# A hand-written order of 946 operations replaced by another, from operation 87 on

## Chip, cores and metric

The kernel runs on one core of one Trainium2 chip. The metric is the device time of one execution in microseconds, as the median of several runs.

## The reference, cut to what matters

Attention with four sink positions and a window of 128, then an MLP whose activation is the square of a relu:

```python
# q, k, v: (4, 8, 768, 64) = batch, heads, sequence, head size; n_sink 4, window 128
scores = q @ k^T / sqrt(64)
keep = (pos_k < 4) | (0 <= pos_q - pos_k < 128)
a = softmax(where(keep, scores, -1e9))
x = (a @ v) as (4 * 768, 8 * 64) = 3072 tokens x 512
h = x @ w_in                # 512 -> 2048
out = (max(h, 0) ** 2) @ w_out    # 2048 -> 512, float32
```

## The kernel before, in words

The work is cut by batch b (0 to 3) and by slab s (0 to 2) of 256 query positions. The heads lie in four pairs m. For a slab, TensorE (PE) makes the scores of two head pairs at a time into two PSUM banks (L613); ScalarE (ACT) takes the exp of each bank (L634); a mask cuts the window's triangles, either on VectorE (DVE, L643 and L646) or on GpSimd (POOL, L218); PE multiplies with the values (L682); DVE normalises (L698 reciprocal, L699 product) into the tile xn_sb. The four sink positions have a small product (L572) and exp (L580) of their own, with "sink values" prepared ahead (L554: four small sums on POOL). The attention output has to be transposed for the MLP. For batches 0 and 1 PE does it (L731, copied out at L192 by ACT or L194 by DVE); for batches 2 and 3 the DMA does it, one tile of 128 positions per issue from SyncE's (SP's) queue (L713, xn_sb to xT). The inputs q and k are also transposed: by PE (L507) for batches 0 and 1, and by DMA from SP's queue (L461, qn to qkT) for batches 2 and 3. POOL's queue issues the loads (L308 w_in, L316 w_out, L372 and L403 q and k, L381 and L415 v). Each queue has eight semaphores for its transfers, so an issue waits until the one eight before it has landed.

The MLP's first layer is done partly in the classic form (L763 products, relu L775 on ACT or L777 on DVE, square L784 or L786) and partly by a scheme with seven instead of eight block products (a "quad", L894): sums of blocks of the input (L852; for some a copy "xd" on ACT, L192, comes first) and of the weights (L810, L818), seven products, and between them partial results t on DVE (L936; the first of them a copy on ACT or DVE), a relu for two of the four blocks (ACT L951 or DVE L953), a fused relu step for the others (L963), squares (ACT L917 or DVE L919). The second layer also goes by sums of squares (L1207), sums of weights (L1025), seven products of eight matmuls each (L1233; classic L984; the last slab has a form of its own, L1094), and its output quarters are copied out (L192, L194) or added (L1247), and stored by SP (L1276).

What sets the order is a table, `ORDER`, at the top of the file: 946 words, one for each operation. `Plan.run` issues the operations in the order of the table. The number of a word names the operation. A letter behind it (p, d, a, g) picks PE, DVE, ACT or POOL for an operation that can run on several, without one it takes the first of its list. `+0` and `+1` pick, for each PSUM slot that the operation takes, the pool "att" or "den"; each has two rooms of two banks. Since each engine works its queue in order, the table fixes the order of every queue, the engine of each movable operation, and which room is free when. A product that takes a room waits for the last reader of what was there.

```python
word, *chosen = word.split("+")
n = int(word.rstrip("pdag"))
o = self.ops[n]
o.engine = names[word[-1]] if word[-1] in names else next(iter(o.engines))
for s in o.takes:
    if len(s.pools) > 1:
        s.pool = s.pools[int(chosen.pop(0))]
    s.room = free[s.pool].pop(0)
o.run(o.engine)
```

The operations that the steps below name, by their number in the table:

| op | what it is |
|---|---|
| 35, 36; 127 | loads of the last two parts of w_out; the making of the masks (POOL) |
| 106, 118 | masks of batch 0, slab 1 |
| 208, 452 | sink values of batches 1 and 2 |
| 128, 166, 171, 282 | transpose of q and k, relu, product of layer 1, product of layer 2, all of batch 0 |
| 183, 184, 185 | last classic product of layer 1, its relu (ACT), its square (DVE) |
| 219, 230; 222, 233, 220, 231 | score products of batch 1; their exps |
| 301; 304, 305 | a sum of squares (DVE); first products of layer 2 of batch 0, slab 2 |
| 369, 383; 271, 273 | relus of two quads; copies of the transposed attention output |
| 389, 390, 408 | xd copy (ACT), sums of it (DVE), first product of a quad that uses them (batch 1, slab 2) |
| 397, 399; 400, 401 | t of a quad; products that need them |
| 454, 459 | sink product of batch 2, an exp |
| 468, 469 | product with the values and norm, batch 2, slab 0 |
| 406, 507 | a fused relu step L963 of a quad, a sum of squares |
| 472, 479 / 495, 488 | score products of batch 2, slab 1 / slab 2 |
| 486, 487, 502, 503; 594 | DMA transposes L713 of batch 2, slabs 1 and 2; sums of xT (L852) that need them |
| 680 to 683 | DMA transposes L461 of q and k of batch 3 |
| 648, 650; 704 | a relu and the product that needs it, batch 2; a score product of batch 3 |

Of the kernel before, what the change touches and what calls it, by code (L numbers as in the profile page):

```python
# [18 lines left out]


ORDER = """
944 0 1 2 7 8 9 10 11 12 13 14 15 16 17 18 945+0 3 5 19 20 21 6 79 22 23 24 25 55d 56d 57+0 58 59d 60a 83+0 85 103+1
105 26 27 28 62d 61d 63+1 64 67d 68d 65a 69+0 70 71d 72d 66a 84+1 73a 74a 75+1 76 78d 91+0 86 77a 93 80 113+1 87+0
92+1 89 94 95+0 97 115 88 90 96 98 114+1 99+0 101 117 100d 104+0 81+1 102d 107 82 4 29 106g 30 31 32 33 34 35 36 37 38
39 40 41 42 43 44 45 46 127 47 48 49 50 116d 118d 108d 156+0 109+1 119+1 121 111 162+0 110 120 122 112 123+1 125 124d
126d 157a 163a 158a 164a 168+1 165+0 51 52 53 54 177+0 169a 170d 208g 166a 167a 178d 171+1 179a 172a 128+1 131+0 174+0
173a 132a 129d 319 323 321 175d 324 176d 322 130a 320 159+1 133a 160a 161a 278+0 279 136+1 144+0 145+0 280 281 148 138
146 289+1 149d 139d 274 147d 275 282 290 283 291 292 284 276 277 134+1 137+0 135 286a 140 141d 285 287d 293 150+0 151
294 142+1 196+0 192+1 295 143 193 200+1 198a 202a 195d 197 199d 201 203d 297d 194d 296 298a 152+1 154 204+0 205
212+0+1 153a 155d 189+0 215 206a 213 190a 214 207d 186+0 216 191d 248+0 187d 249d 251+1 209 253a 188d 252a 180+1 181d  # L30
250d 182d 183+0 326 184a 185d 300 301 230+0+1 233 299 288 219+0+1 231 220 304+0 210+0 306a 211 222 305 237+0+0 240
232d 325 302 221 303 223 241d 238 239d 311 307 217+1 254+0 224+0 308a 255 309 218 242+0 225 243 452g 422 423 424 425
426 427 428 429 430 431 432 433 434 234g 235+1 226+0 228 310a 227a 229a 314 236 244+0 246 316a 247a 327 313 245d 329
256+0+1 257 315 328 332 317 330 347+1 333+1 348 334 259 335a 337 312 336 331 338 349a 263+1+1 266 264 339 351 340 341a
350 352 435 436 437 258g 438 439 267g 265g 361+0 353 362 354 363d 260g 364 343 365 366 445 440 453 444 441 355a 356a
342a 448 446 449 442 447 443 451 450 318 344 345 357 375+0 358 376 261+0 359 377a 346a 367 368 379 378 262 380 268+0
# [6 lines left out]
477+0 500+0 485 478 559 501 561 527+0 528 529d 563 562 493+0 565 558d 494 534 530 535 531d 566+0 567 532 533a 568d 569  # L43
564 570 572 571 536 683 682 677 678 486 502 680 711+0+0 487 503 573 574d 537 538 539d 540 681 541 560 714 712 704+0+0
580+0 581 576 577 582d 583 594 584 585 575a 705 707 688+0+0 713g 715g 706g 708g 689 691 578 586 587 626+1 627 588a
628a 612+0 686+0 613 687 630 596 692 690 595 629 631 716+0 717 589a 614a 632 633 579a 634a 635a 615 590 616 597 617
693+0 694 591 618 636 619 637 592 598+1 599 620a 600a 638 593a 601 622 640+0 641 602 623 642a 736 643 603 644 604 646
605 645 709+0 647 624 740+0 639a 621a 606a 648a 742a 649a 607a 608 609 738 737 650 651 743 739 710 610 611d 741
695+0+0 744a 625a 696 698 652 653d 755 697 699 756 757 745 747 746a 749 748 720+0+0 723 759+0 750 700+0 701 761a 762
751 721 752a 763a 760 722g 753 724g 727+0+1 774 775 758 728 730 725+0 766 764 778+1 779 765a 729d 767 776 726 777 768  # L50
731g 732+1 733 718 719 702 703 754 734 735 793 794 785 770 769 798+1 812+0 799 813 780a 771a 800a 814a 781 782a 797
796 786 772 795 815 801 802 816 817 818 803 783 819 784d 787 820a 804 805 789 822 823 829 826 827 828 791 806a 807a
821a 808 809 788 830+0 831 790a 832a 824 825d 810 858+1 811a 834 872+0 844+1 860a 846a 874a 833 835 836 837 873 845
859 876 838a 839a 886 887 888 875 877 861 840 841 848 862 864 792 773 842 863 847 889 849 878 879 890+0 865 843a 880a
850 882 883 851 892a 881a 866d 867d 884 893 894d 868 869 852a 853a 854 855 870 856 895 891 897 896a 885a 900 857d 871d
905 909+1 899 907 901 924 926 906 898 925 903 911a 912 913a 902a 928+1 904 914 910 929 931+1 915d 908 927 918 920 919
930a 933a 916 922 921d 934 917 923 932 935 936 939 937 938 943 940 942 941
"""
DUMMIES = {
    945: 29, 58: 8, 63: 10, 64: 4, 83: 3, 91: 3, 97: 3,  # L60
# [1340 lines left out]
```

## Time and profile before

| | us |
|---|---|
| runs shown | 210.41, 210.48, 211.18 |
| median | 210.48 |
| profiled execution, first to last instruction (span) | 208.3 |
| median less span | 2.2 |
| DVE busy | 173.1 |
| ACT busy | 135.9 |
| POOL busy | 96.4 |

The profile shows one execution. The span runs from its first to its last instruction. A line of a group names the source line, the engine, the operation, the tile written and the tiles read, the count, and then the busy time in all, the mean of one in ns, and the engine's idle time just before them with what ended it. A line of the windows gives, for a stretch of time, the busy time of each engine in the order PE, PEld (weight loads, beside PE), DVE, ACT, POOL, with the count of instructions, then the granted clock, the DMA share and the rate. A line of the waits gives who waited for whom, the time in all, how often, and the longest. In a timeline, the square bracket holds the idle time ahead of the row and what ended it.

### The profile page before, as it was taken

To read this page: it belongs to the slowest core of one execution; us is meant where nothing else is said; L and a number is where in the kernel's file an instruction comes from. 1 tells how busy PE (TensorE), PEld (TensorE's weight loads), DVE (VectorE), ACT (ScalarE), POOL (GpSimd) and SP (SyncE) were. 2 spreads that over 40 slices of the span, in tenths; PEclk is the share of its full clock that TensorE was granted. 3 is DMA by queue.
4 is the path that set the end of the run, shared out by engine and by line. 5 is a ranking of instruction groups with operands and counts; after the bars stand their busy time and mean duration, and the time that the engine had idled before them with its cause. 6 is when DMAs were issued, how large, how long until landed. Compare 5 with 4: busy or idle time off the path is not lost.

```text
span 208.3 us, 5924 instructions
## 1 busy us (share of the span) xinstructions
PE 200.5 (96%) x2476; PEld 174.3 (84%) x2476; DVE 173.1 (83%) x318; ACT 135.9 (65%) x189; POOL 96.4 (46%) x138
## 2 busy tenths in 40 slices
PE   7989999999998999999999998999999999999993
PEld 7658997457986889989878987999888999998893
DVE  6759268867599998999999987999989598999933
ACT  2695888433749589999987047988856248693110
POOL 7999274599599976689356209000043000000000
PEclk9999999999999999999999999999999999999999
DMA  6999999999999999999999945300204203200115
GB/s 190 260 184 207 173 196 215 166 146 142 261 68 148 131 172 137 181 162 121 154 116 220 109 96 134 148 3 0 50 14 145 50 5 113 88 3 0 50 54 201
DMA packets 93994, 26.10 MB, mean 125 GB/s; under 512 B 86800, under 2 KB 91408, under 8 KB 93968
## 3 DMA queue, kind: packets, MB, share of 16 engines
q0 software_dynamic: 69248, 12.59, 80.2%
q1 hardware_dynamic: 24536, 13.01, 27.9%
q8 instruction: 19, 0.31, 0.6%
q10 hardware_dynamic: 184, 0.14, 0.2%
q14 instruction: 7, 0.06, 0.1%
HBM read 27.30 MB, written 6.29 MB: 161 GB/s over the span
## 4 chain that ended last, share of the span: by engine, by line
PE 82%; DVE 5%; DMA 4%; SPq 3%; ACT 2%; issue 2%; DVEq 0%; ACTq 0%
PE py L1233 26%; PE pm L894 23%; PE pm L763 10%; PE py L984 7%; PE po L682 6%; PE ps L613 4%; DMA qr<-in_q_dram 3%; PE pt L507 2%; PE py L1094 2%; SPq L351 2%; DVE t L936 1%; PE px L731 1%; DMA xT<-xn_sb 1%; SPq L461 1%; ACT expm L634 1%
## 5 line engine op out<-in xcount | busy, mean ns | idle before, releaser
L634 ACT ACTIVATE expm<-ps 128x1024 bf16<-128x1024 f32 (+1 forms) x48 | 43.7, 953 | 7.7 <-PE ps L613 7.5
L218 POOL TENSOR_SCALAR_AFFINE_SELECT expm<-expm 128x512 bf16<-128x512 bf16 x34 | 22.7, 705 | 44.2 <-ACT expm L634 40.4
L894 PEld LDWEIGHTS <-w_in_sb 128*128 128x128 bf16 x384 | 32.2, 114 | 2.0 <-issue 1.9
L1233 PEld LDWEIGHTS <-gT_sb 128*128 128x128 bf16 x288 | 27.2, 98 | 4.7 <-issue 1.4
L917 ACT ACTIVATE gT_sb<-r 128x1024 bf16<-128x1024 bf16 x28 | 28.8, 1054 | 2.5 <-DVE r L963 2.3
L894 PE MATMUL pm<-xs,wi 128*128 128x256 bf16 (+1 forms) x288 | 29.2, 246 | 0.1
L192 ACT ACTIVATE osb<-py 128x256 f32<-128x256 f32 (+1 forms) x30 | 11.9, 399 | 25.0 <-PE py L1233 19.8
L936 DVE TENSOR_TENSOR t<-t,pm 128x512 f32<-128x512 f32 x36 | 23.8, 683 | 3.7 <-PE pm L894 2.9
L894 PEld LDWEIGHTS <-wi 128*128 128x128 bf16 x288 | 24.6, 114 | 1.0 <-DVE xs L852 0.4
L1233 PEld LDWEIGHTS <-sg 128*128 128x128 bf16 x216 | 20.3, 98 | 2.7 <-issue 0.5
L963 DVE CUSTOM_DVE_ANT_1 r<-pm,t 128x1024 bf16<-128x1024 f32 x18 | 21.8, 1218 | 0.5 <-PE pm L894 0.5
L763 PE MATMUL pm<-xT,w_in_sb 128*128 128x256 bf16 x192 | 22.0, 273 | 0.0
L763 PEld LDWEIGHTS <-w_in_sb 128*128 128x128 bf16 x192 | 20.6, 114 | 0.3 <-issue 0.2
L894 PE MATMUL pm<-xs,w_in_sb 128*128 128x256 bf16 (+1 forms) x192 | 19.9, 246 | 1.0 <-DVE t L936 1.0
L951 ACT ACTIVATE r<-pm 128x1024 bf16<-128x1024 f32 x16 | 16.3, 1022 | 4.9 <-DVE osb L194 2.3
L1233 PE MATMUL py<-w_out_sb,gT_sb 128*128 128x256 bf16 x144 | 18.7, 273 | 0.6 <-ACT expm L634 0.6
L1233 PE MATMUL py<-wt,sg 128*128 128x256 bf16 x144 | 18.7, 273 | 0.0
L1233 PE MATMUL py<-wt,gT_sb 128*128 128x256 bf16 x144 | 18.5, 273 | 0.0
L682 PEld LDWEIGHTS <-expm 128*128 128x128 bf16 x352 | 16.6, 97 | 1.9 <-issue 0.6
L682 PE MATMUL po<-v,expm 128*128 128x65 bf16 x352 | 17.8, 193 | 0.3 <-ACT expm L634 0.3
L699 DVE TENSOR_TENSOR xn_sb<-po,rc 128x512 bf16<-128x512 f32 (+1 forms) x28 | 17.2, 615 | 1.0
L984 PE MATMUL py<-w_out_sb,gT_sb 128*128 128x512 bf16 x64 | 14.8, 379 | 0.0
(104 smaller groups left out, 376.9 us busy)
## 6 DMA issues: line engine op xcount, KB each, us to landing
out_dram<-osb SPq DMA_DIRECT2D x11, 512.0 KB, 3.7
v<-in_v_dram POOLq DMA_DIRECT2D x24, 128.0 KB, 6.2
qn<-in_k_dram POOLq DMA_DIRECT2D x20, 128.0 KB, 6.1
qn<-in_q_dram POOLq DMA_DIRECT2D x20, 128.0 KB, 6.5
w_in_sb<-in_moe_w_in_dram POOLq DMA_DIRECT2D x4, 512.0 KB, 9.4
w_out_sb<-in_moe_w_out_dram POOLq DMA_DIRECT2D x4, 512.0 KB, 10.8
qr<-in_k_dram SPq DMA_DIRECT2D x4, 256.0 KB, 5.1
qr<-in_q_dram SPq DMA_DIRECT2D x4, 256.0 KB, 4.8
```

The source lines that it names most:

```text
L218: nc.gpsimd.affine_select(out=e_tile, in_=e_tile, compare_op=ALU.is_ge, fill=fill, base=i - 1, pattern=[[0, n], [1 if i else -1, 128]], ch ...
L634: nc.scalar.activation(out=x[:, :, o:512], in_=bank_t["s", b, s, m][:, :, o:512], func=AF.Exp, scale=scale)
L682: touch(("po", b, s, m0), e, nc.tensor.matmul(pv[:, i, h2, :], lhsT=lhsT, rhs=rhs, start=(n_ == 0), stop=(n_ == len(mms) - 1)), j)
L699: touch(("po", b, s, m0), e, nc.vector.tensor_tensor(out=xn_sb[:, 2 * s:2 * s + 2, 128 * (m0 + j0):128 * (m0 + j0 + nj)].rearrange("p i (j ...
L763: nc.tensor.matmul(pm[:, i, :], lhsT=w_in_sb[:, fb // 4, kb, fb % 4:512:4], rhs=xT[:, c0 // 256:(c0 + cw) // 256, kb, :], start=(kb == 0), ...
L894: touch(tag, e, nc.tensor.matmul(y[:, bk, i, :], lhsT=weights(name, f0 + i, a), rhs=rhs[:, a, :], start=fresh and i == 0 and a == 0, stop= ...
L917: nc.scalar.activation(out=d, in_=x, func=AF.Square)
L936: touch(tag, e, nc.vector.tensor_tensor(out=T["t"], in0=T["t"], in1=T["y"][:, bk], op=ALU.subtract), bk)
L951: touch(tag, e, nc.scalar.activation(out=r, in_=T["y"], func=AF.Relu), 0, 1)
L963: touch(tag, e, nc.vector._custom_dve(TENSOR_ADD_SAT, out=r.rearrange("p b n c -> p b (n c)"), in0=T["y"].rearrange("p b n c -> p b (n c)" ...
L984: touch((b, u), e, nc.tensor.matmul(pm[:, i, :], lhsT=gT_sb[:, fb, 128 * t:128 * t + 128], rhs=w_out_sb[:, fb, :], start=(fb == 0), stop=( ...
L1233: touch((b, u), e, nc.tensor.matmul(region(name), lhsT=x[:, i, :], rhs=w_[:, i, :], start=first and i == 0, stop=i == HB - 1, skip_group_c ...
```

## The change

Only `ORDER` changes. Its first 86 words name the same operations in the same order. Behind them stand the same operations as before in another order; 58 of them run on another engine (masks: four from DVE to POOL, seven from POOL to DVE; output quarters: seven from ACT to DVE, six from DVE to ACT; sink values 208 and 452 from POOL to DVE; the rest are relus, squares, first t's and copies between ACT and DVE), and some products take another pool. The table has one line less, so that each line number behind it is lower by one in the changed kernel. PE has 2476 products in both. Cut to the rows that are spoken of (the old ones first):

```diff
-92+1 89 94 95+0 97 115 88 90 96 98 114+1 99+0 101 117 100d 104+0 81+1 102d 107 82 4 29 106g 30 31 32 33 34 35 36 37 38
-39 40 41 42 43 44 45 46 127 47 48 49 50 116d 118d 108d 156+0 109+1 119+1 121 111 162+0 110 120 122 112 123+1 125 124d
...
-250d 182d 183+0 326 184a 185d 300 301 230+0+1 233 299 288 219+0+1 231 220 304+0 210+0 306a 211 222 305 237+0+0 240
...
-270+0 381 382 360a 369a 271a 269 370d 371 272 273d 372 383a 389 373 463+0+0 385 386 466 464 390 408+0 409 394+1 395
-410a 391 393 387 411 396a 397 412 456+1+0 413 392 414 398 400 415 374d 388a 457 384a 399 504 458 506 465 467 505 508+0
-416a 401 418 419 510a 511 402a 654 655 684g 656 657 658 659 660 661 662 663 664 665 672 459 420 460 685 512a 417a 421a
-403a 404 468+0 509 405 513 454+1 469 406 507 514a 455 515 461+0 472+1+0 407a 517 523 542 462 518 519 521 544 675 673
-470 473 546+0 475 543 548a 479+0+0 516 520d 549 480 482 550a 524 481d 545 476d 525 483d 547 495+1+0 551 553 496 552a
-498 556 674 676 666 667 668 474g 669 670 499g 471 522 679 488+0+0 555 554 526 497d 484+1 557 491 489 671 492g 490g
...
-564 570 572 571 536 683 682 677 678 486 502 680 711+0+0 487 503 573 574d 537 538 539d 540 681 541 560 714 712 704+0+0
-580+0 581 576 577 582d 583 594 584 585 575a 705 707 688+0+0 713g 715g 706g 708g 689 691 578 586 587 626+1 627 588a
...
+89 94 95+0 97 115 88 90 96 98 114+1 99+0 101 117 100 104+0 102 4 29 106 118 30 81+1 156+0 31 82 107 109+1 32 33 116d
+34 108d 110 119+0 120 111 121 162+1 157 112 122 123+0 125 168+1 127 124a 126 158 35 159+0 169 177+1 170 178d 165+0 36
+128+0 163 179a 208d 129 164a 166d 37 174+1 130a 131+0 38 39 175 171+0 160d 278+0 40 279 161a 132a 319 145+0 176 41
...
+54 189+0 248+0 215 207a 250a 190 299 324 251+0 252a 186+0 187 321 191 180+0 183+0 181 209 184 326 325 422 452d 216 253
+188 249 219+0+1 423 182 222 424 185 300 301 328 230+0+1 304+0 233 220 231 425 210+1 305 306 211 302 426 223 427 232d
...
+367 261+0 377 359 378 356a 267 379 346a 366 268+0 368 684 381 360a 369 262 270+0 380 382 269 371 272 370 654 271a 383
+451 372 273 389 463+0+0 373 390 466 385 386 408+0 387 318 410 394+1 395 374 391 464 409 655 411 392 396 412 413
+456+1+0 656 397 398 388a 457 384a 414 393 657 415 400 508+0 416 399 504 506 505 458 459 401 418 454+0 419 509 510 511
+658 402 404 460 659 420 455 417a 507 467 512 405 675 465 513 403a 461+1 660 661 468+0 662 514 421a 406 663 407a 515
+469 462 664 472+0+0 473 542 518 544 546+0 677 475 548 516 517 474d 673 476d 679 479+0+0 549 519 470 480 665 482
+495+0+0 471 543 521 666 523 672 483 547 550 520 498 674 496 553 481d 488+0+0 525 484+1 491 551 499d 485 552d 522 555
+497 477+0 545 478 527+0 489 490d 557 556 558d 561 667 524 559 492 529 554 563 500+0 668 493+0 685 678 562 676 530 526
+566+0 494 567 531 501 568 532 486 528 487 711+0+0 570 569 565 533d 502 669 712 537 503 571 714 572 536 704+0+0 564 707
+682 573 705 538 539d 715d 534 688+0+0 689 574d 594 540 683 681 576 577 691 713 680 626+1 535 578 627 580+0 692 581 596
```

More of the change, by code (lines that the diff above doesn't have):

```diff
@@ L32 @@
[L32 to L36, printed above, removed]
@@ L57 @@
[L57 removed]
+944 0 1 2 7 8 9 10 11 12 13 14 15 16 17 18 945+0 3 5 19 20 21 6 79 22 23 24 25 55d 56d 57+0 58 59 60a 83+0 85 103+1
+105 26 27 28 62d 61d 63+1 64 67d 68d 65a 69+0 70 71 72 66a 84+1 73a 74a 75+1 76 78 91+0 86 77a 93 80 113+1 87+0 92+1
+89 94 95+0 97 115 88 90 96 98 114+1 99+0 101 117 100 104+0 102 4 29 106 118 30 81+1 156+0 31 82 107 109+1 32 33 116d
+34 108d 110 119+0 120 111 121 162+1 157 112 122 123+0 125 168+1 127 124a 126 158 35 159+0 169 177+1 170 178d 165+0 36
@@ new lines @@
+590 591 631 632 598+1 592 633 599 579a 600 640+0 593a 634 617 597 641 736 601 618 619 642 602 620 636 644 621a 643 637
+604 603 622 638 623 646 706 605 645 647 624 737 635a 709+0 738 740+0 639a 606 608 625a 609 648 650 742d 710 651 718
+670 743 610 649a 607a 695+0+0 541 744 698 741 671 652 745 720+1+0 739 696 699 611a 697 746d 723 700+0 749 750 701 751
+721 653 702 747 755 724 727+0+0 759+0 756 760 730 722d 753 703 757 719 748 728 752d 729d 778+1 761 754 793 731d 774
+794 725+0 762 726 732+1 733 763 764 766 798+1 734 800 812+0 813 799 795 775 780 776 796 814d 801 781 802 767 765 816
@@ new lines @@
+782 783 815 768 817 804 803 818 819 735 784d 826 770 779 805 758 777 820 769 829 797 822 806 823 771 827 787 772 788
+824 821a 808 830+0 831 832d 872+0 785 828 873 874 807 809 789 790 875 833 876 834 810 786 836 791 835 877 844+1 825a
+846 811a 845 858+1 773 837 878 860 838 859 847 848 879 861 862 839a 886 863 849 840 841 842 864 880 881a 888 889 865
+882 850 851 866 890+0 868 883 887 843 867a 884 792 869 870 852 891 853a 854 855 892 885a 893 856 897 894 871a 895 857
+905 907 896 909+0 900 924 899 925 902d 911 912 913 901 908 928+1 903 929 914 915 898 904 926 906 910 931+0 918 930d
@@ L58 @@
+916 919 920 934 933 927 932 935 922 936 917 939 937 938 921 940 923 943 942 941
 """
```

28 lines of the change are left out of this document (9 added, 19 removed).

## The prediction

> **What bounds the kernel now.** The page comes first: who is busy, and whether anything throttles.
>
> ```profile
> span 208.3 us, 5924 instructions
> PE 200.5 (96%) x2476; PEld 174.3 (84%) x2476; DVE 173.1 (83%) x318; ACT 135.9 (65%) x189; POOL 96.4 (46%) x138
> ...
> PEclk9999999999999999999999999999999999999999
> DMA  6999999999999999999999945300204203200115
> ...
> q0 software_dynamic: 69248, 12.59, 80.2%
> ```
>
> TensorE (PE) is busy in 96% of the span at full clock, so a new order can win only the time in which PE waits, less what lies outside its reach at the two ends. The median of the runs, 210.48, is 2.2 above the span; I take that as constant. The windows show where PE's idle time lies (columns: PE, PEld, DVE, ACT, POOL, clock, DMA share, GB/s).
>
> ```profile
> 60.00:66.00 6.00, 5.02 (x64) 3.60 (x62) 5.88 (x11) 4.89 (x8) 6.00 (x8) 1.00 2.12 135
> ...
> 88.00:92.00 4.00, 3.85 (x56) 3.20 (x54) 3.99 (x8) 3.81 (x6) 2.67 (x3) 1.00 1.63 201
> 92.00:112.00 20.00, 20.00 (x269) 16.90 (x266) 19.78 (x37) 17.88 (x26) 12.54 (x17) 1.00 2.19 135
> ...
> 125.00:131.00 6.00, 5.03 (x83) 4.50 (x84) 4.54 (x7) 4.48 (x6) 4.71 (x8) 1.00 0.60 172
> ...
> 200.00:208.30 8.30, 4.96 (x54) 4.37 (x51) 3.37 (x9) 0.26 (x1) 0.00 (x0) 0.99 0.35 126
> ```
>
> Behind the kept start there are three stops: 0.98 us at 60 to 66, 0.15 at 88 to 92, 0.97 at 125 to 131, together 2.1; the last window's 3.3 is the closing store. So no order can gain much more than 2.1: 208.4 is the floor. The waits of PE name who ended the stops.
>
> ```profile
> PE pm L894 <- DVE t L936: 1.0, 1, 1.0
> PE py L1233 <- ACT expm L634: 0.6, 1, 0.6
> ...
> PE ps L613 <- ACT r L775: 0.4, 1, 0.4
> ```
>
> The stop of 1.0 has its cause further back, in SyncE's queue. The chain of waits around it:
>
> ```profile
> 121.64 0.52 SPq L713
> ...
> 122.25 2.03 SPq L461
> ...
> 124.34 1.26 SPq L713
> ...
> 125.65 2.50 DMA xT<-xn_sb
> ...
> 129.14 0.69 DVE t L936
> ...
> 129.87 1.92 PE pm L894 x20
> ```
>
> L713 transposes the attention output xn_sb into xT, one tile per issue. Between the issues of op 502 (ended 122.16) and ops 487 and 503 stands a transpose of another batch's input (L461, op 680), which holds SP for 2.03 us; the last landing comes at 128.15, DVE's sums of xT (op 594) wait for it, and behind 594 in DVE's order waits the t that PE needs at 129.87.
>
> **The change part by part.** PE gets the same 2476 products, so I first added up PE's durations in both orders, with nothing waiting: a product of L1233 is eight matmuls, of L894 four or eight. The two sums differ by 0.1 us in favour of the new order (a score or sink product, with its short contraction, costs about 0.1 more at a change to the others, and both have the same number of changes): **-0.1**. Everything else is waits. To find them I took the new order at this clock and asked, of each engine's queue, whether the work between two dependencies of PE fits into what PE does meanwhile. The durations for it:
>
> ```profile
> L634 ACT ACTIVATE expm<-ps 128x1024 bf16<-128x1024 f32 (+1 forms) x48 | 43.7, 953 | 7.7 <-PE ps L613 7.5
> ...
> L1233 PE MATMUL py<-w_out_sb,gT_sb 128*128 128x256 bf16 x144 | 18.7, 273 | 0.6 <-ACT expm L634 0.6
> ...
> L936 DVE TENSOR_TENSOR t<-t,pm 128x512 f32<-128x512 f32 x36 | 23.8, 683 | 3.7 <-PE pm L894 2.9
> ...
> L963 DVE CUSTOM_DVE_ANT_1 r<-pm,t 128x1024 bf16<-128x1024 f32 x18 | 21.8, 1218 | 0.5 <-PE pm L894 0.5
> ```
>
> (1) *The stop at 129.9.* In the new table 486, 487, 502 and 503 stand together ahead of 682, 683, 681 and 680. Op 503 then follows 502 by one issue of 1.26 us, lands 2.5 us after its start, and by my walk is there about 2 us before PE asks for the sums. Nothing else late appears at this place: **-1.0**. If the move failed to clear it, the term is 0.
>
> (2) *The stop at 60 to 66* stays. The rows:
>
> ```profile
> 62.10 0.34 PE L613 MATMUL ps<-qkT 64*128 64x256 bf16 x4 [0.40 <-ACT r L775]
> 63.02 1.03 PE L1233 MATMUL py<-w_out_sb,gT_sb 128*128 128x256 bf16 x8 [0.57 <-ACT expm L634]
> ...
> 61.03 1.02 ACT L775 ACTIVATE r<-pm 128x1024 bf16<-128x1024 f32 x1 [2.63 <-PE pm L763]
> 61.95 2.64 ACT L634 ACTIVATE expm<-ps 128x1024 bf16<-128x1024 f32 x3
> ```
>
> PE has just ended its last product of the classic form (op 183); the relu 184 follows it (1.02), then three exps, and the first product of layer 2 needs the square 185 behind that relu. In both tables 184 heads ACT's queue, the exps 222, 233, 220 and 231 follow in another order, PE has the same two score products in between, and the next product waits for DVE's sum 301 behind 185 in both. By these durations the queue's work exceeds PE's by 1.14 us in the one and the other: **0** (0 to +0.2).
>
> (3) *88 to 92.* ACT's copy xd (op 389) comes behind the relu 383 and DVE's copy 273, and op 408 needs the sums 390 of it. The walk of the new order: relu 369 ends at 85.85 on the stall-free clock, copy 271 at 86.4, relu 383 at 87.45, 389 at 88.5, 390 at 88.85, against PE's 88.40; the same chain as before, a little later: **+0.15** (0 to +0.3).
>
> (4) *92 to 112.* This is the place that decides. DVE has 19.78 busy of 20 us here in the old order, and PE does not wait. Two things tighten. First, the norm 469:
>
> ```profile
> 99.92 0.69 DVE L699 TENSOR_TENSOR xn_sb<-po,rc 128x512 bf16<-128x512 f32 x1
> 100.52 1.22 DVE L963 CUSTOM_DVE_ANT_1 r<-pm,t 128x1024 bf16<-128x1024 f32 x1
> 101.66 0.68 DVE L1207 TENSOR_TENSOR sg<-gT_sb,sg 128x1024 bf16<-128x1024 bf16 x1
> ...
> 102.52 0.61 PE L613 MATMUL ps<-qkT 64*128 64x128 bf16 x12
> ```
>
> The score product 472 (at 102.52) had 0.78 us to spare behind the r of L963 (op 406, ended 101.74). The new table puts the sum 507 (0.68, some 0.60 in a full queue) and then 406 ahead of the norm 469, and 472 takes the banks of both: its first half waits for 406, its second half, 0.27 later, for 469. The 0.78 goes, and by the walk about 0.25 is missing: between 0, where DVE's queue alone would put it, and 0.5. On the way there the t of op 397 is 0.14 late for product 400, and the exp 459 0.07 late for 454: together 0.45.
>
> Second, the four score products of slabs 1 and 2 (472, 479, 495, 488) now take both rooms of one pool each (+0+0), where 472 and 495 had one room of each pool (+1+0). So each waits for both exps of the one before:
>
> ```profile
> 103.25 1.94 ACT L634 ACTIVATE expm<-ps 128x1024 bf16<-128x1024 f32 x2
> ...
> 106.23 1.94 ACT L634 ACTIVATE expm<-ps 128x1024 bf16<-128x1024 f32 x2
> ```
>
> 1.94 and two handovers of 0.05 make 2.04; between them PE has two products of layer 2, 2 x 0.87 and 0.1: 1.85. That is 0.19 too little for a whole product, but the second exp frees only the second half, which PE reaches 0.27 later: 0.08 to spare, three times. I count nothing, and 0.3 at worst, if ACT starts each pair 0.2 late. The stretch: **+0.45** (0 to 1.1).
>
> (5) *After 112.* The same turn at 704 is covered in the same way. The relu 648 at 143 comes 0.2 after product 650 could start: **+0.2** (0 to 0.5). From 150 to 200 no queue's work exceeds PE's by over 0.1. The tail keeps its last product, copies and stores: 0 (-0.2 to +0.2).
>
> (6) *Engines and POOL's queue.* 58 operations change engine. The sums stay near: seven masks leave POOL for DVE and four go the other way (+3 x 0.68 on DVE), two sets of sink values go to DVE, 13 output quarters swap between ACT and DVE. Two costs are not in the old trace. The sink values on DVE are four small sums; they took 0.40 each on POOL, where the whole operation held 1.65 to 1.9 us, and the nearest DVE row is 0.42 for 128x256: between 0.6 and 1.9, I take 1.3, and at that the wait of 171 for relu 166 at 31.7 does not appear; at 1.9 it costs 0.4. And POOL now makes the masks (2.35 us) ahead of the issue of the last two parts of w_out, and mask 118 (1.23) ahead of five loads:
>
> ```profile
> 24.77 0.54 POOL L316 DMA_DIRECT2D w_out_sb<-in_moe_w_out_dram  x1 [2.63 <-DMA w_in_sb<-in_moe_w_in_dram]
> ...
> w_out_sb<-in_moe_w_out_dram POOLq DMA_DIRECT2D x4, 512.0 KB, 10.8
> ```
>
> A load of w_out lands 10.8 us after its issue, because much is queued ahead of it (the DMA digits are 9 from 5 to 115 us, and POOL's queue, q0, alone takes 80.2%). An issue that comes 2 us later still joins a queue that is not empty, so the landing moves little: 0 (0 to +1.0). By the landings of the old trace every load has at least 0.7 us of slack in the new order.
>
> [...]
>
> ```profile
> L218 POOL TENSOR_SCALAR_AFFINE_SELECT expm<-expm x34: 629/638/1169, 16.2 to 159.1; 128x512 bf16<-128x512 bf16 x34
> ...
> L646 DVE TENSOR_TENSOR expm<-expm,tri x15: 679/685/1117, 16.5 to 157.9; 128x1024 bf16<-128x1024 bf16 x15
> ```
>
> Most of both run at their least, and a few take 0.4 to 0.5 more. [...]
>
> **The sum.** 210.48 - 0.1 - 1.0 + 0 + 0.15 + 0.45 + 0.2 = 210.18; I say **210.1**, as (4) counts the small misses one upon the other, though a late PE gives the queues back some of it. (On the profiled execution: 208.3 - 0.4 = 207.9, and 2.2 around it.) With (2) to (5) at their lower ends it is 209.4, at their upper ends 211.5.
>
> **Rivals.** *A, faster:* the stop at 129.9 goes, and the small misses of (3) to (5) disappear, because PE's stop at 62 gives DVE and ACT a lead that my stall-free clock does not give them, and each later miss gives it again. Then 210.48 - 0.1 - 1.0 = 209.4, less the 0.15 of 88 to 92 and up to 0.4 of the stop at 62: 208.8 to 209.4. For it: the old order shows 20.00 of PE in 92 to 112 at the same load of DVE, and none of the new misses is above 0.25. Against: DVE's queue between 397 and 469 is longer by 507. *B, slower:* DVE sets the pace from 87 to 112. With 19.78 busy of 20 it has no reserve, so each wait of DVE for ACT or PE (the xd copy, the first t of a product) shifts PE one for one. My walk finds 1.0 of such gaps from 87 to 93, of which the sum counts 0.45; if all arrive at 472, if the exps of the four score products each start 0.4 late for it, past their 0.08 (3 x 0.32), and if two masks that changed sides collide at 0.4, the price is 0.55 + 0.96 + 0.4 = 1.9: 212.0 (211.6 to 212.8). It decides from the point where norm 469 ends more than 1 us behind its product 468. *C, slower:* a load issued behind POOL's masks finds its queue empty, and op 282 or 128 waits by up to the 2 us that the issue comes later: 211.6 to 212.1. Against it stand the 10.8 us of queue.
>
> **How the numbers follow.** A measurement of this kernel can tell about 0.5%, 1.05 us, from no change: 209.4 to 211.5. The forecast has 0.40, all within that; A has 0.33, and I count it as faster, though its upper end only touches the bound; B has 0.21 and C 0.06, both slower. So faster 0.33, same 0.40, slower 0.27. The range reaches to the low end of A and over C into the upper half of B, and leaves out the rest: 208.8 to 212.5.
>
> **What would show it.** (1) is right if PE's wait for t at L936 of 1.0 us is gone and the L713 issues 486 to 503 stand together, ended before 122. (2): PE's waits for L634 and L775 near 61 to 64 remain, about 1.0 together. (4): one wait of PE of some 0.2 for norm (L699) or L963 at 472, and none for the exps of the four score products. (5): one wait of 0.2 for a relu. Wrong would be: a wait of PE for a DMA (C), waits for DVE or ACT of over 1 us together between 88 and 112 (B), no waits there at all (A), or an L936 wait of 1.0 as before.

## The result, and the profile after

The changed kernel took **213.07 us** (median of four runs, 212.58 to 213.50), the kernel before 210.64 (four runs, 210.41 to 211.18). The ratio is **1.011** with an interval of 1.007 to 1.015: slower by 1.1%, where 210.1 with a range of 208.8 to 212.5 was forecast. In the changed kernel each line number is lower by one: L893 is the former L894, L645 the former L646, and so on.

The page of the changed kernel, profiled at 212.58:

```profile
span 210.9 us, 5902 instructions
...
PE 201.6 (96%) x2472; PEld 174.7 (83%) x2476; DVE 180.7 (86%) x330; ACT 135.9 (64%) x188; POOL 89.7 (43%) x124
```

The span is 2.6 longer; the granted clock was 1.000 in both. DVE has 12 instructions and 7.6 us more; the forecast had moved three more masks of 0.68 and two sets of sink values at 1.3 each to it, 4.6 in all. The other 3.0 must lie in longer instructions, and the groups say which ones (minimum, median and maximum in ns stand behind the count; one view for the masks, one for the t):

```profile
L645 DVE TENSOR_TENSOR expm<-expm,tri x18: 675/685/2169, 16.8 to 159.7; 128x1024 bf16<-128x1024 bf16 x18
```

```profile
L935 DVE TENSOR_TENSOR t<-t,pm x36: 675/681/689, 78.1 to 184.3; 128x512 f32<-128x512 f32 x36
```

The 18 masks take 16.2 in all, 5.1 more than the 15 of before, of which three masks of 0.68 explain 2.0. The longest took 2.17, against 1.12 before; not one of the 36 t is longer than 0.69. The windows show where PE pays (columns as before: PE, PEld, DVE, ACT, POOL, clock, DMA share, GB/s):

```profile
16.00:22.00 6.00, 5.47 (x90) 4.82 (x88) 5.85 (x13) 3.12 (x4) 5.99 (x8) 1.00 1.24 206
60.00:66.00 6.00, 4.90 (x56) 3.90 (x54) 5.88 (x14) 5.09 (x8) 6.00 (x8) 1.00 2.15 145
80.00:84.00 4.00, 3.26 (x29) 2.94 (x28) 3.63 (x5) 1.99 (x2) 1.19 (x3) 1.00 2.13 136
88.00:93.00 5.00, 4.79 (x60) 3.95 (x57) 4.77 (x9) 4.81 (x6) 4.61 (x7) 1.00 0.84 89
125.00:131.00 6.00, 6.00 (x83) 5.18 (x81) 5.57 (x10) 4.22 (x5) 4.48 (x7) 1.00 0.45 88
```

Two of these stretches were full in the kernel before:

```profile
16.00:22.00 6.00, 6.00 (x101) 5.70 (x100) 5.09 (x14) 2.98 (x5) 4.88 (x7) 1.00 1.24 207
80.00:84.00 4.00, 4.00 (x53) 3.86 (x52) 3.28 (x4) 3.91 (x8) 1.93 (x5) 1.00 1.79 195
```

The stop of 125 to 131 is gone (6.00 of 6), as forecast. In its place PE idles 0.53 at 16 to 22 and 0.74 at 80 to 84, where the prediction had no term at all. The waits of PE name the releasers:

```profile
PE pm L893 <- DVE t L935: 0.7, 1, 0.7
PE po L681 <- DVE expm L645: 0.5, 1, 0.5
PE py L1232 <- DVE gT_sb L1206: 0.4, 1, 0.4
PE ps L612 <- DVE qkT L193: 0.4, 1, 0.4
...
PE py L1232 <- ACT expm L633: 0.3, 1, 0.3
...
PE pm L893 <- ACT r L950: 0.2, 1, 0.2
```

PE's records overlap (in the changed kernel one of 0.23 starts at 18.73 and the next at 18.79), so the idle time understates a stop. To add the stops up I took, for each product, the time from the start of the one before to its own start, less the median of that time for products of the same kind; what is left is its stop. Behind op 104 these stops come to 3.0 in the kernel before and 5.3 in the changed one: +2.3. PE's last matmul ends at 204.96 and at 207.54, 2.6 apart; the rest is 0.4, by which op 104 started later, less the 0.1 of PE's own work. That 0.4 lies in the part that both tables share. It is the first 82 words, not 86, and op 104 is the last of them: it starts at 16.01 in the kernel before and at 16.40 in the changed one, and anywhere from 16.2 to 18.1 in the runs below. So the 0.4 belongs to the execution, not to the order.

| stop at product (us) | before | after | forecast for after |
|---|---|---|---|
| 111 (20.1), behind masks 116 and 108 | 0 | 0.65 | 0 |
| 354 (82.4), behind mask 265 and t 352 | 0 | 0.85 | 0 |
| 230, 304, 305 (62 to 66) | 1.20 | 1.37 | 1.20 |
| 408 and 371 (90 to 93) | 0.31 | 0.54 | 0.46 |
| 400, 454, 472 (96 to 106) | 0 | 0.25 | 0.45 |
| 587 (129.9) | 1.05 | 0 | 0 |
| 650 (148.2) | 0 | 0.40 | 0.20 |
| 189, 244, 340, 893 in all | 0 | 0.75 | 0 |
| 357, 901 in all | 0.28 | 0 | 0.28 |

The first two rows hold 1.5 of the excess. What DVE and POOL did there (start, length, engine, line; DVE first):

```profile
16.85 3.20 DVE L645 TENSOR_TENSOR expm<-expm,tri 128x1024 bf16<-128x1024 bf16 x2
...
78.10 2.08 DVE L935 TENSOR_TENSOR t<-t,pm 128x512 f32<-128x512 f32 x3
80.10 1.65 DVE L645 TENSOR_TENSOR expm<-expm,tri 128x1024 bf16<-128x1024 bf16 x1
81.67 0.68 DVE L935 TENSOR_TENSOR t<-t,pm 128x512 f32<-128x512 f32 x1
```

```profile
16.65 2.86 POOL L217 TENSOR_SCALAR_AFFINE_SELECT expm<-expm 128x512 bf16<-128x512 bf16 x4
...
77.57 3.62 POOL L217 TENSOR_SCALAR_AFFINE_SELECT expm<-expm 128x512 bf16<-128x512 bf16 x6
```

Two masks of DVE that take 0.68 each at their median last 3.20 beside the four mask instructions of POOL (ops 106 and 118), and the mask 265 takes 1.65 where POOL makes masks until 81.19. The three t that run before it beside the same POOL instructions take their ordinary 0.69. PE resumes just behind:

```profile
20.11 0.24 PE L681 MATMUL po<-v,expm 128*128 128x65 bf16 x2 [0.49 <-DVE expm L645]
...
82.39 0.60 PE L893 MATMUL pm<-xs,w_in_sb 128*128 128x256 bf16 x4 [0.69 <-DVE t L935]
```

### The profile page after: what moved, and what is told of

It is laid out like the page before. It is cut to its first block, busy times and chain, and to the rows that moved or that the text cites. A ratio compares the mean times of both kernels' runs of the same rounds, so it can differ in the third digit from the quotient of the medians.

```text
span 210.9 us, 5902 instructions
## 1 busy us (share of the span) xinstructions
PE 201.6 (96%) x2472; PEld 174.7 (83%) x2476; DVE 180.7 (86%) x330; ACT 135.9 (64%) x188; POOL 89.7 (43%) x124
## 4 chain that ended last, share of the span: by engine, by line
PE 69%; DVE 15%; ACT 7%; DMA 3%; issue 2%; SPq 2%; ACTq 0%; DVEq 0%
PE py L1232 22%; PE pm L893 19%; PE pm L762 8%; PE py L983 7%; PE po L681 5%; PE ps L612 4%; DMA qr<-in_q_dram 3%; DVE expm L645 3%; ACT r L950 3%; ACT gT_sb L916 2%; PE pt L506 2%; PE py L1093 2%; SPq L350 2%; ACT expm L633 1%; DVE t L935 1%
## 5 line engine op out<-in xcount | busy, mean ns | idle before, releaser
L633 ACT ACTIVATE expm<-ps 128x1024 bf16<-128x1024 f32 (+1 forms) x48 | 43.2, 953 | 7.5 <-PE ps L612 7.3
L217 POOL TENSOR_SCALAR_AFFINE_SELECT expm<-expm 128x512 bf16<-128x512 bf16 x28 | 20.4, 772 | 41.7 <-ACT expm L633 31.8
L893 PEld LDWEIGHTS <-w_in_sb 128*128 128x128 bf16 x384 | 32.4, 114 | 2.0 <-issue 1.9
L916 ACT ACTIVATE gT_sb<-r 128x1024 bf16<-128x1024 bf16 x30 | 31.0, 1056 | 0.3
L893 PE MATMUL pm<-xs,wi 128*128 128x256 bf16 (+1 forms) x288 | 29.2, 246 | 0.5 <-ACT r L950 0.2
L893 PEld LDWEIGHTS <-wi 128*128 128x128 bf16 x288 | 24.5, 114 | 1.9 <-issue 1.2
L935 DVE TENSOR_TENSOR t<-t,pm 128x512 f32<-128x512 f32 x36 | 23.7, 682 | 2.3 <-PE pm L893 1.9
L191 ACT ACTIVATE osb<-py 128x256 f32<-128x256 f32 (+1 forms) x28 | 10.8, 396 | 20.1 <-PE py L1232 14.5
L1232 PEld LDWEIGHTS <-sg 128*128 128x128 bf16 x216 | 20.1, 98 | 2.8 <-issue 0.7
L950 ACT ACTIVATE r<-pm 128x1024 bf16<-128x1024 f32 x17 | 17.4, 1023 | 6.4 <-PE pm L893 6.2
L893 PE MATMUL pm<-xs,w_in_sb 128*128 128x256 bf16 (+1 forms) x192 | 19.7, 246 | 0.7 <-DVE t L935 0.7
L645 DVE TENSOR_TENSOR expm<-expm,tri 128x1024 bf16<-128x1024 bf16 x18 | 16.2, 915 | 2.2 <-ACT expm L633 2.2
```

Source lines behind the costliest of these rows:

```text
L217: nc.gpsimd.affine_select(out=e_tile, in_=e_tile, compare_op=ALU.is_ge, fill=fill, base=i - 1, pattern=[[0, n], [1 if i else -1, 128]], ch ...
L633: nc.scalar.activation(out=x[:, :, o:512], in_=bank_t["s", b, s, m][:, :, o:512], func=AF.Exp, scale=scale)
L645: nc.vector.tensor_mul(y, y, tri.rearrange("p (o a) c -> p o (a c)", o=1).to_broadcast([128, 4, 256]))
L893: touch(tag, e, nc.tensor.matmul(y[:, bk, i, :], lhsT=weights(name, f0 + i, a), rhs=rhs[:, a, :], start=fresh and i == 0 and a == 0, stop= ...
L916: nc.scalar.activation(out=d, in_=x, func=AF.Square)
L935: touch(tag, e, nc.vector.tensor_tensor(out=T["t"], in0=T["t"], in1=T["y"][:, bk], op=ALU.subtract), bk)
```

## The experiments

**The theory:** the new table puts masks of DVE beside masks of POOL, where DVE's instruction takes longer (a collision: 2.17 and 1.65 above, at a median of 0.68), and at two places the next thing that PE needs is that mask or stands behind it in DVE's queue. **The rival:** nothing collides that matters; DVE's queue has simply become longer, by the operations that it took over, and is late by its ordinary durations. Another rival gives the time to the many small waits for ACT and DVE in (2) to (5). Each ratio is to the kernel before, timed together with the run; the base is the kernel that the run's edit starts from. For runs 1 to 3 the interval of the ratio overlaps that of the changed kernel (1.007 to 1.015), so there the stops of the profiles carry the argument, not the times.

**1. The early masks all on DVE** (base: the changed kernel). This gives DVE two masks more, so that the rival would have more of its cause, and the theory none.

```diff
-89 94 95+0 97 115 88 90 96 98 114+1 99+0 101 117 100 104+0 102 4 29 106 118 30 81+1 156+0 31 82 107 109+1 32 33 116d
-34 108d 110 119+0 120 111 121 162+1 157 112 122 123+0 125 168+1 127 124a 126 158 35 159+0 169 177+1 170 178d 165+0 36
+89 94 95+0 97 115 88 90 96 98 114+1 99+0 101 117 100 104+0 102 4 29 106d 30 81+1 156+0 31 82 107 109+1 32 33 116d 34
+108d 118d 110 119+0 120 111 121 162+1 157 112 122 123+0 125 168+1 127 124a 126 158 35 159+0 169 177+1 170 178d 165+0
```

> The changed kernel with masks 106 and 118 on VectorE, so that all four masks of batch 0, slab 1 run there (order 106, 116, 108, 118) and GpSimd makes none of them. Theory collision (a two-input mask on VectorE and a mask on GpSimd shut each other out): the two masks at 16.8 that took 3.20 us together shrink to about 0.68 each, PE's wait of 0.5 at 20.1 (0.65 by the starts of its products) goes, 0.5 to 0.7 us less than the changed kernel: 212.3 to 212.6. Rival queue (VectorE simply has too much to do there): two more masks on it add up to 1.3, the wait grows to about 1.2 to 2, 213.6 to 214.4.

Measured: 212.1, ratio 1.007 (1.0045 to 1.010). DVE's timeline:

```profile
16.64 1.28 DVE L645 TENSOR_TENSOR expm<-expm,tri 128x1024 bf16<-128x1024 bf16 x2
...
18.22 1.29 DVE L645 TENSOR_TENSOR expm<-expm,tri 128x1024 bf16<-128x1024 bf16 x2 [0.30 <-ACT expm L633]
```

Four masks in 2.6, where two had taken 3.2, and the stop at 111 is gone; every other stop is as in the changed kernel (their sum is 4.64 instead of 5.32). More work on DVE and less waiting: at this place it is the collision and not the queue, for which 213.6 or more was expected.

**2 and 3. Mask 265 later on DVE, and on POOL** (base: the changed kernel).

```diff
-351 453 339 443 340 353 445 265d 352 362 341 354 343 449 355 448 363d 258 344 375+0 450 357 358 342a 364 376 365 345
+351 453 339 443 340 353 445 352 362 341 354 343 449 355 448 363d 258 344 375+0 450 357 358 342a 364 265d 376 365 345
```

> The changed kernel with mask 265 still on VectorE, but behind t 364 in the table, after GpSimd's three masks have ended. Theory collision: the mask takes 0.68 in place of 1.64, PE's wait of 0.7 for t at 82.4 goes with the smaller one before it (1.07 by the starts of products), nothing is paid later: about 1.0 less, 212.0 to 212.2. Rival queue: the work is the same, only moved by some 1.3 us; it takes 0.6 off the stop at 82.4 and pays part of it back at the products that need 363 to 367: 0.2 to 0.5 less, 212.6 to 212.9.

Measured: 211.69, ratio 1.006 (1.003 to 1.009). DVE's timeline and POOL's:

```profile
78.01 2.67 DVE L935 TENSOR_TENSOR t<-t,pm 128x512 f32<-128x512 f32 x4
...
82.25 0.69 DVE L645 TENSOR_TENSOR expm<-expm,tri 128x1024 bf16<-128x1024 bf16 x1
```

```profile
77.48 3.62 POOL L217 TENSOR_SCALAR_AFFINE_SELECT expm<-expm 128x512 bf16<-128x512 bf16 x6
```

Four t run 2.67 beside six mask instructions of POOL, unslowed; the mask behind them takes 0.69, and 354's stop of 0.85 is gone (the 0.22 at 340 stays).

The same execution also shows that a collision need not come out the same way twice. The early part of the table is that of the changed kernel, but here POOL comes to its masks at 17.29, behind the start of DVE's mask 116:

```profile
16.94 0.72 DVE L645 TENSOR_TENSOR expm<-expm,tri 128x1024 bf16<-128x1024 bf16 x1
18.52 0.76 DVE L645 TENSOR_TENSOR expm<-expm,tri 128x1024 bf16<-128x1024 bf16 x1 [0.86 <-ACT expm L633]
```

DVE's two masks are hardly stretched. PE does not stop at 111; it stops for 0.48 at product 121 instead, where it waits for POOL's mask 118, which is late.

```diff
-351 453 339 443 340 353 445 265d 352 362 341 354 343 449 355 448 363d 258 344 375+0 450 357 358 342a 364 376 365 345
+351 453 339 443 340 353 445 265g 352 362 341 354 343 449 355 448 363d 258 344 375+0 450 357 358 342a 364 376 365 345
```

> The changed kernel with mask 265 on GpSimd, as it was before. Theory collision: 1.0 less than the changed kernel, as with the late mask, 212.0 to 212.2, unless the values product 261 waits for GpSimd's mask 258, which comes 1.23 later (bound +0.3). Rival queue: one mask of 0.68 less on VectorE, 0.6 to 0.7 less: 212.4.

Measured: 212.06, ratio 1.007 (1.004 to 1.010); the same stop is gone. Both runs show that 354 waits because mask 265 stands ahead of t 352. That it is the mask's stretching and not its presence follows by arithmetic alone: it took 0.96 over its median, more than the whole stop.

**4. The transpose 680 behind 503** (base: the kernel before). This is part (1) of the change by itself.

```diff
-564 570 572 571 536 683 682 677 678 486 502 680 711+0+0 487 503 573 574d 537 538 539d 540 681 541 560 714 712 704+0+0
+564 570 572 571 536 683 682 677 678 486 502 711+0+0 487 503 680 573 574d 537 538 539d 540 681 541 560 714 712 704+0+0
```

> The kernel before with one word moved: the transpose 680 of q and k behind 503, so that the four transposes of the attention output (486, 487, 502, 503) meet it no more. Theory: the stop of 1.0 at 129.9 goes and nothing takes its place, 0.9 to 1.05 less than before: 209.6. Rival: another wait takes its place (680 or 681 late for batch 3, or the sums 594 wait for 503 anyway): less than 0.3 gained, 210.4 to 210.6.

Measured: 209.74, ratio 0.997 (0.995 to 0.9994). The window of the old stop:

```profile
125.00:131.00 6.00, 6.00 (x93) 5.33 (x91) 5.01 (x10) 5.28 (x7) 4.93 (x8) 1.00 0.69 204
```

PE is full, and the sum of the stops falls from 3.0 to 1.9. The times show 0.6 of it, less than the 0.9 to 1.05 expected.

**5. Mask 118 on POOL behind 106** (base: the kernel before): the early collision put in alone. The old order already has a smaller one there: its three masks on DVE take 2.55 beside POOL's mask 106, in place of 2.0.

```diff
-92+1 89 94 95+0 97 115 88 90 96 98 114+1 99+0 101 117 100d 104+0 81+1 102d 107 82 4 29 106g 30 31 32 33 34 35 36 37 38
-39 40 41 42 43 44 45 46 127 47 48 49 50 116d 118d 108d 156+0 109+1 119+1 121 111 162+0 110 120 122 112 123+1 125 124d
+92+1 89 94 95+0 97 115 88 90 96 98 114+1 99+0 101 117 100d 104+0 81+1 102d 107 82 4 29 106g 118g 30 31 32 33 34 35 36
+37 38 39 40 41 42 43 44 45 46 127 47 48 49 50 116d 108d 156+0 109+1 119+1 121 111 162+0 110 120 122 112 123+1 125 124d
```

> The kernel before with one mask moved: 118 from VectorE to GpSimd, right behind mask 106. This puts one of the two collisions of the new table into the old one. Theory collision: VectorE's mask 116 has to sit out GpSimd's mask instructions and takes about 2 in place of 0.91, mask 108 behind it 1.1 in place of 0.68, product 111 waits 0.4 to 0.65 on L646: 0.4 to 0.65 slower than before, though VectorE has one mask less to do. Rival queue: VectorE's queue is shorter by 0.68, nothing gets slower: 0 to 0.1 faster.

Measured: 210.9, ratio 1.002 (0.999 to 1.0055), which doesn't tell it from no change. DVE's timeline, then POOL's:

```profile
17.55 3.19 DVE L646 TENSOR_TENSOR expm<-expm,tri 128x1024 bf16<-128x1024 bf16 x2
```

```profile
17.35 2.85 POOL L218 TENSOR_SCALAR_AFFINE_SELECT expm<-expm 128x512 bf16<-128x512 bf16 x4
```

The stretching is there to the hundredth (3.19 beside 2.85). The price is smaller than expected: a stop of 0.28 at 111, where 0.4 to 0.65 was expected. Exps, sums and products stand in another order around it there; which of these gives PE the rest of the time, the run doesn't show.

**6. All masks apart that had met, or so I thought** (base: the changed kernel): the edits of runs 1 and 2, and mask 239 on DVE.

```diff
-428 237+0+0 238 307 221 288 240 311 429 303 430 224+1 308 254+0 255 241d 431 217+0 432 442 239 309 234 225 242+0 433
+428 237+0+0 238 307 221 288 240 311 429 303 430 224+1 308 254+0 255 241d 431 217+0 432 442 239d 309 234 225 242+0 433
```

> The changed kernel with all three meetings of masks taken out: 106, 118 and 239 on VectorE, 265 behind t 364. Theory collision: the stops of 0.65 at 20.1, 0.85 at 82.4 and the 0.19 at 73.9 (norm 236, behind masks that met 239 and 234) go: 1.7 less than the changed kernel, 211.0 by the ratio to before +0.3%. Rival: the stops come back at the next product, because VectorE has three masks of 0.68 more (2.0): less than 1.0 gained, 211.7 or more.

Measured: 212.46, ratio 1.009 (1.006 to 1.013): the gain did not come. The stops at 20 and 82 are gone, and a new one of 1.41 stands at product 307. PE's waits, DVE's timeline and POOL's:

```profile
PE py L1232 <- DVE sg L1206: 1.3, 1, 1.3
```

```profile
65.71 1.98 DVE L1206 TENSOR_TENSOR sg<-sg,gT_sb 128x1024 bf16<-128x1024 bf16 x1
```

```profile
65.82 1.31 POOL L217 TENSOR_SCALAR_AFFINE_SELECT expm<-expm 128x512 bf16<-128x512 bf16 x2
```

In the changed kernel POOL makes 239 and 234 from 68.2 on. With 239 off POOL, mask 234 ran at 65.8, just as DVE made the sum 302, which takes 0.69 elsewhere and took 1.98. The collision had moved to a sum that PE waits for. The expectation failed, and the theory gained: another instruction was stretched, and PE stood for it. Not all of the delay is explained, though: the sum of weights just ahead (op 328, L817) took 1.12 in place of 0.68, and POOL's rows show only the issue of a load beside it.

**7. Run 6 with three operations moved**: the sink product 454 behind product 419, relu 648 ahead of the square 625, relu 369 ahead of the square 360.

```diff
-367 261+0 377 359 378 356a 267 379 346a 366 268+0 368 684 381 360a 369 262 270+0 380 382 269 371 272 370 654 271a 383
+367 261+0 377 359 378 356a 267 379 346a 366 268+0 368 684 381 369 360a 262 270+0 380 382 269 371 272 370 654 271a 383
...
-456+1+0 656 397 398 388a 457 384a 414 393 657 415 400 508+0 416 399 504 506 505 458 459 401 418 454+0 419 509 510 511
+456+1+0 656 397 398 388a 457 384a 414 393 657 415 400 508+0 416 399 504 506 505 458 459 401 418 419 454+0 509 510 511
...
-604 603 622 638 623 646 706 605 645 647 624 737 635a 709+0 738 740+0 639a 606 608 625a 609 648 650 742d 710 651 718
+604 603 622 638 623 646 706 605 645 647 624 737 635a 709+0 738 740+0 639a 606 608 648 625a 609 650 742d 710 651 718
```

> As the one without meetings, and three single waits of the new table undone besides: relu 648 ahead of square 625, relu 369 ahead of square 360, sink product 454 behind product 419. If the list of stops is complete, these take away 0.40, 0.23 and 0.25 more: 0.9 less than the kernel without meetings, 210.1 to 210.3, level with or just under before. Rival: each only moves to the next product, because ScalarE and VectorE are full there: 0 to 0.4 less.

Measured: 212.93, ratio 1.012 (1.008 to 1.015). PE's waits:

```profile
PE py L1232 <- DVE sg L1206: 1.4, 1, 1.4
...
PE pm L893 <- ACT r L950: 0.6, 1, 0.6
```

The 0.25 at 454 and the 0.40 at 650 are gone, so those two are waits for one operation in the wrong place. The swap at 369 only pushed the wait on: 0.72 at 385. And the collision of run 6 is still there.

**8. Run 4 with the transposes 251 and the sinks' work moved off the stop at 62** (base: the kernel before).

```diff
-212+0+1 153a 155d 189+0 215 206a 213 190a 214 207d 186+0 216 191d 248+0 187d 249d 251+1 209 253a 188d 252a 180+1 181d
-250d 182d 183+0 326 184a 185d 300 301 230+0+1 233 299 288 219+0+1 231 220 304+0 210+0 306a 211 222 305 237+0+0 240
+212+0+1 153a 155d 189+0 215 206a 213 190a 214 207d 186+0 216 191d 248+0 187d 249d 209 188d 180+1 181d 250d 182d 183+0
+251+1 253d 252d 184a 185d 300 301 326 230+0+1 233 299 288 219+0+1 231 220 304+0 210+0 306a 211 222 305 237+0+0 240
```

> The kernel before with 680 behind 503 (as in the run with that word alone), and with the transposes 251 put behind the last classic product 183, their copies on VectorE ahead of square 185, and the sum 326 behind 301: 0.45 of PE's work now lies in the stop at 62. Theory: that stop falls from 1.20 to about 0.75, and with the 1.0 of the transposes of the attention output the kernel is 1.4 to 1.5 under before: 209.0. Rival: the copies of 251 delay square 185 or score product 219, and the 0.45 is paid back: 209.4 to 209.6.

Measured: 214.79, ratio 1.021 (1.017 to 1.026), at a granted clock of 0.984 in the profiled execution. PE's waits:

```profile
PE po L682 <- POOL expm L218: 2.6, 2, 2.2
```

The stop at 62 did not shrink (0.75 at 219 and 0.85 at 304), and 3.2 of stop came at product 226, which waits for a mask on POOL. In POOL's order loads that wait for the moved transposes stand ahead of that mask; I had not asked who is queued behind them.

**9. Mask 265 on DVE ahead of 352** (base: the kernel before), as the changed kernel has it.

```diff
-350 352 435 436 437 258g 438 439 267g 265g 361+0 353 362 354 363d 260g 364 343 365 366 445 440 453 444 441 355a 356a
+350 265d 352 435 436 437 258g 438 439 267g 361+0 353 362 354 363d 260g 364 343 365 366 445 440 453 444 441 355a 356a
```

> The kernel before with the other meeting of the new table put in: mask 265 on VectorE ahead of t 352, while GpSimd makes masks 258, 267 and 260. Theory collision: it starts at 79.2, when exp 264 has ended, takes 1.1 to 1.7 in place of 0.68, and product 354 waits 0.8 to 1.3 for t 352: 0.6 to 1.2 slower than before. Rival queue: it takes 0.68, the late start alone makes product 354 wait 0.3: 0.3 slower at most.

Measured: 211.06, ratio 1.003 (1.001 to 1.005). DVE's timeline:

```profile
79.55 0.89 DVE L646 TENSOR_TENSOR expm<-expm,tri 128x1024 bf16<-128x1024 bf16 x1 [0.67 <-ACT expm L634]
```

There is a stop of 0.97 at 354, but for another reason: here the mask waits 0.67 for its exp, and beside POOL's masks (78.67 to 81.52) it takes only 0.89. So this run can't give the collision's size. It shows something else: the stop at 587 shrank from 1.05 to 0.46, since the last landing of the transposes does not wait for PE; a delay ahead of it is partly given back. What is left of that stop is no wait for a landing. DVE goes straight on to the sum 594, which takes 0.91 in place of 0.42 beside masks of POOL (126.0 to 130.9):

```profile
128.94 0.91 DVE L852 TENSOR_TENSOR xs<-xT 128x512 bf16<-128x512 bf16 x1
```

**10. Five masks apart and two operations moved** (base: the changed kernel): run 6 with mask 234 on DVE as well, and the moves of 454 and 648 of run 7.

```diff
-428 237+0+0 238 307 221 288 240 311 429 303 430 224+1 308 254+0 255 241d 431 217+0 432 442 239 309 234 225 242+0 433
+428 237+0+0 238 307 221 288 240 311 429 303 430 224+1 308 254+0 255 241d 431 217+0 432 442 239d 309 234d 225 242+0 433
```

> The changed kernel with 106, 118, 234 and 239 on VectorE (so that no mask of GpSimd is left there to meet the sums of squares, as 234 met 302 in the run before), 265 late, relu 648 ahead of square 625 and sink product 454 behind 419; the relu 369 is left where the new table has it. Theory collision: no stop at 20, 67.8 or 82; the stops left after 16 us are those of 62 to 66 (1.4), 80 (0.2), 90 to 93 (0.5), 191 (0.2), and 0.2 at 74: some 2.7 against 3.0 of before, 210.0 to 210.5, level with before within 0.3%. Rival: two masks more on VectorE make it late at 68 to 75, 0.5 or more slower than before.

Measured: 211.32, ratio 1.002 (0.999 to 1.0045), against 1.011 (1.007 to 1.015) for the changed kernel: the two intervals do not meet. The windows of the two collisions:

```profile
16.00:22.00 6.00, 5.96 (x97) 5.40 (x97) 5.55 (x15) 3.42 (x5) 3.09 (x4) 1.00 1.25 206
80.00:84.00 4.00, 3.94 (x38) 3.78 (x35) 3.51 (x6) 2.65 (x3) 1.00 (x2) 1.00 1.65 144
```

Both are nearly full again, though DVE makes four masks more than in the changed kernel, and the sum of the stops is 3.7 (5.3 there). That is 1.0 more than the 2.7 expected. The two collisions account for 1.5 of the fall and the two moved operations for 0.65; against that, the products 235, 226 and 244 at 71 to 74 now stop for 0.7 (0.2 in the changed kernel), at the place where the rival had expected DVE to be late. What is left besides is the stretch of 62 to 66 (1.4), 408 as in the kernel before (0.31), and small waits of 0.1 to 0.25 at other products.

**11. Run 4 again, measured more often**, as the version to keep.

> The kernel before with 680 behind 503 once more, with more rounds, as the version to keep: 0.9 to 1.0 less than before (its profile has lost that stop and gained none), ratio 0.995 to 0.996; if the first measurement was the truth, 0.997.

Measured: 209.75 (209.00 to 211.38, 12 runs), ratio 0.997 (0.995 to 0.9994). SyncE's queue:

```profile
117.51 2.56 SPq L461 DMA_TRANSPOSE qkT<-qn  x2
120.17 5.97 SPq L713 DMA_TRANSPOSE xT<-xn_sb  x4
126.24 2.53 SPq L461 DMA_TRANSPOSE qkT<-qn  x2
```

The four transposes of xn_sb run as one block and end at 126.1. The version is faster than the kernel before by 0.3%, a gain of 0.6 as in run 4 and not the 0.9 to 1.0 expected; by the two intervals it is also faster than the changed kernel.

## Why the prediction was wrong

- **(1) The stop at 129.9**: right. It is gone in the changed kernel, and alone (run 4) it is worth 1.05 of stop, but only 0.6 of time. The block of issues stands together, though it ends at 125.8, not ahead of 122: the whole table is later by some 2.9 there, and its second half waits for the norm 501 (ended 122.89). But the reading of the old stop gave all of it to SyncE's queue. DVE's row in the kernel before shows two parts:

```profile
128.27 0.95 DVE L852 TENSOR_TENSOR xs<-xT 128x512 bf16<-128x512 bf16 x1 [0.64 <-DMA xT<-xn_sb]
```

DVE waits 0.64 for the landing; then the sum 594 itself takes 0.95, where its median is 0.42, beside masks of POOL that last from 124.77 to 129.71. So a collision of 0.53 stood on PE's path already in the old order. In run 4 both parts are gone (the sum takes 0.48 there); in run 9 the wait is gone and the collision stays.
- **(2) 60 to 66**: nearly right in size, 1.37 for 1.20, but by luck: the waits are others than forecast: DVE's copy of L193 for the scores (0.4), the exp, and the sum of L1206 (0.4), in place of the relu.
- **(3) 88 to 92**: right in size (0.54 for 0.46), but the place was not. At 408, where I put the +0.15, nothing changed (0.31); the new 0.23 is product 371, whose relu 369 stands behind the square 360.
- **(4) 92 to 112**: too high, 0.25 for 0.45. The 0.25 at product 472 did not come. Product 454, counted at 0.07, waited 0.25 for its exp. The four score products with both rooms in one pool wait nowhere, as costed. So the place that "decides", and rival B's condition for it, decided nothing: DVE's 19.8 of 20 was no bound.
- **(5) 648**: the mechanism was right, the size 0.40 for 0.20.
- **(6) Engines and POOL's queue**: no load came late, so rival C had no part. But **the step that failed** is the one on the masks that change sides. The forecast shows their rows, a few of them 0.4 to 0.5 longer than the rest, and its sum has no term for them: I took 0.5 as the most that a new neighbour does to a single mask, and held that PE does not wait for those masks. Both halves fell. Mask 116 took 1.48 more than its median, 265 took 0.96 more, and they stood ahead of what PE needs next: 0.65 and 0.85 of stop, 1.5 in all. The second half did not even hold for the old order, where the sum 594 of (1) was such a case. The 0.5 was about the largest excess of the old order, that is, of an order in which long meetings had been few; I took it for a property of the instruction, and did not lay DVE's masks over POOL's in the new order. Rival B had the kind of cost in it (two masks that collide, at 0.4, where the changed kernel's two had 1.48 and 0.96 of excess) and came near with its total (212.0, at most 212.8, for 213.07), but by other terms.

Against the forecast the stops are 2.5 too many. The two collisions give 1.5, product 650 gives 0.2, the stretch of 62 to 66 another 0.2, products 189, 244, 340 and 893 together 0.75, and (3) gives 0.1. Two small stops of before that did not come back take off 0.3, and (4) takes off 0.2. Some 0.3 lies in pieces too small to name. At the places that (2) to (5) name, the stops were 0.25 above the forecast in total; the walk saw the size of the small waits better than their places.

What the runs show: undoing the early collision takes its stop away (run 1), undoing both collisions together with two misplaced operations brings the kernel from 1.011 to 1.002 (run 10), and one collision, moved by accident, costs as much elsewhere (run 6). What stays open: how much of 354's 0.85 a mask of ordinary length would leave (run 9 met another wait), why the same meeting cost 0.65 in one table and 0.28 in another, what the early collision costs on average over executions of one table (0.65 in the changed kernel's profile, 0.43 in run 3's, and in run 2's the other way round), and what sets the small waits at 189, 244, 340 and 893, which no run took away.

## What to carry to other kernels

A new order changes not only when an operation's inputs are there, but what runs beside it: before costing a table, lay the DVE operations that were stretched here (the masks, the sums of squares, the sums of xT) over POOL's masks, and reckon with more than one POOL instruction: the excess reached 1.48 beside a back-to-back run of 2.86 and 1.30 beside one of 1.31. Most of the masks' meetings cost less (0.43 at the median). A largest excess seen in the old order is no bound for a new one. And a stop that a queue sets from outside (here SyncE's transposes) gives back part of what is lost ahead of it (in run 9 the one at 587 fell from 1.05 to 0.46), so stops are not simply added.

## What the runs showed of the hardware

DVE's masks and some of its sums took longer beside masks of POOL. In the profiles of the kernel before and the changed one, 10 of DVE's 33 masks of L646 (L645 in the changed kernel) ran beside a computation of POOL and took up to 2.17; none of the other 23 took over 0.69. The sums of squares of L1207 (L1206) took up to 1.12 there and 0.69 at most elsewhere; the sums of xT of L852 (L851), 128x512, up to 0.95 there and 0.42 elsewhere. POOL's masks were stretched too: eleven of its mask instructions took 1.08 to 1.17, each beside such an operation of DVE, and those that met none took 0.72 at most. Two more things came out that I had not expected.

*The stretching can be more than one POOL instruction.* A mask beside four mask instructions of POOL, three of them of 0.64 to 0.65, took 2.17, and a sum took 1.98 beside two (1.31 together): their excess of 1.48 and 1.30 is more than one POOL instruction. Over the 13 traces of this case the masks of L645 that ran beside a POOL computation (44 of them) were longer by 0.43 at the median and by 1.48 at most, and the sums of L1206 by up to 1.30. But a meeting need not cost that much: mask 265 in run 9 took only 0.89 beside four of POOL's, and in run 2 the mask 116, which had started first, took 0.72. The sum of 1.12 in run 6, with no computation of POOL beside it by the profile, stays unexplained.

*Two operations with an operand in PSUM were not slowed.* The t of L935, whose second operand is pm in PSUM, met POOL 98 times in these traces and was never longer by more than 0.01; nor was L1246, 94 times (line numbers of the changed kernel). In the row of run 2, four of the t run in 2.67 beside six mask instructions of POOL. These operations also work on float32 and the stretched ones on bfloat16, so the runs do not tell which of the two matters. So here, which DVE operation stands beside POOL's work mattered more than how much.
